# Folding the keys into the query weight in 16 pieces instead of 64, with a new hand-written order of all engines

## The chip, the core and the metric

The kernel runs on one NeuronCore of a Trainium2 chip. The metric is the device time of one execution in microseconds (us). Five engines work side by side: PE (TensorE, matmuls; its weight loads are listed as PEld), DVE (VectorE), ACT (ScalarE), POOL (GpSimd), and SP (SyncE), which here issues every DMA. A matmul reads a stationary operand (the weight) and a moving operand from SBUF and writes PSUM.

## The reference, cut to what matters

S = 2048 tokens of D = 576 features pass through four blocks, A, B, A, B, each with a layer norm in front and a residual sum behind. Both A blocks use the same weights, and so do both B blocks.

```
def A(x):                                   # linear attention, 32 heads of 18
    q, k, v = x @ wqkv
    phi = lambda t: where(t > 0, t + 1, exp(t)) + 1e-6
    kv = phi(k)^T v ;  z = sum over tokens of phi(k)     # per head
    return ((phi(q) kv) / (phi(q) z + 1e-6)) @ wo
def B(x):                                   # 32 heads, 2 x 8 keys of 128, one of 64 experts per head
    q = x @ w_q                             # (tokens, 32, 256)
    s1 = q[..., :128] @ k1.T ; s2 = q[..., 128:] @ k2.T  # 8 scores each
    e = argmax(s1) * 8 + argmax(s2)
    return sum over heads of gelu(x . u[e]) * v[e]
x = x + A(ln(x)); x = x + B(ln(x)); x = x + A(ln(x)); x = x + B(ln(x))
```

The kernel never forms the query of block B. It multiplies w_q by the keys once (the **fold**): 64 blocks of w_q (2 halves of 32 heads, each 128 x 576) times the keys give one 576 x 448 score weight, whose columns are the scores of keys 1 to 7 less that of key 0. Both B blocks use it.

## The kernel before, in words

**Tiles.** The tokens are 16 tiles of 128. For each of the two layers (A and B together, l = 0 and 1) a *front* goes over all tiles: layer norm, transposition (`fT`), and the products with wqkv for k, v and q, each 28 matmuls, because float32 is split into a high and a low part; `st` adds phi(k)^T v of the tile to the state in PSUM. After tile 15 the state is masked (`mk`), summed (`zs`) and multiplied into wo (`M0` to `M4`). Then a *back* goes over all tiles: `num` (POOL and DVE: phi(q) over its denominator), `oT` (transposition), `O` (28 matmuls with the folded wo, residual sum, layer norm), `bT` (transposition), `S` (14 matmuls with the score weight, written into the tile `pps`), `gel` and `sel` (gelu and selection, on ACT, POOL and DVE), `cT` (transposition of the chosen weights, `pc`), and `po` (4 matmuls with v and the residual sum). Most transpositions go through DVE and a round trip to DRAM; a few are on PE. Some q products are left for the back (`q`, or `lq` in layer 1).

**Order.** Nothing is scheduled at run time. A long text is played (`play`, line 719): each word, such as `q0.5` or `F0.12`, names a piece (kind, layer, tile or number), and runs its generator on to its next `yield`; `x2` means two steps. `in_order` (line 136) then ties the instructions of each of PE, ACT, DVE, POOL and SP into the order of the text. So each engine's queue is strictly that order, and a waiting instruction holds back all behind it on its engine.

**The fold.** `wf0.m` (`fold_load`, line 581) issues on SP the load of weight block m (288 KB) into a stage buffer. Stage buffers come in a ring of ten (`RING`, line 110; the tags are shared with tiles of the back), the first 15 uses being the loads of wqkv, so block m waits until block m - 10 has been used. `F0.m` (`fold_mm`, line 585) multiplies one block by the padded keys `kpad`: block m = 16 ch + 4 a + j writes rows 32j to 32j+31 of the PSUM tile `fold_ps` number ch, in two matmuls of 320 and 256 columns. Each is float32 and shows in the trace as two matmul records, so one block is four records. The window of `kpad` shifts with a, so that four a's accumulate into the same rows. `Fo` (ACT) copies a finished chunk ch out, and `FT` transposes and splits it into the score weight `shi`, `slo`; `S` needs all four chunks.

Of the kernel before, what the change touches and what calls it, by code (L numbers as in the profile page):

```python
# [63 lines left out]
def network(ctx, tc, x_in, wqkv, wo, wq_t, k_t, u_t, v2, c_mask, c_mask4, c_ident, c_code, c_code1, c_scale, c_shift, out):  # L64
    nc = tc.nc
# [519 lines left out]
    def fold_mm(l, m):  # L585
        st = fold_st.pop(m)
        ch, i = divmod(m, 16)
        if i == 0:
            fold_ps[ch] = psum(f"fold_ps{ch}")
        p = fold_ps[ch]  # L590
        a, j = divmod(i, 4)
        for c0, c1, at in ((0, 320, 0), (320, D, 512)):
            nc.tensor.matmul(p[32 * j:32 * j + 32, at:at + c1 - c0], kpad[:, ch // 2, 24 - 8 * a:56 - 8 * a],  # L593
                             st[:, c0:c1], start=(a == 0), stop=(a == 3))
# [134 lines left out]
    with in_order(*ALL, ET.SP):  # L729

        play("""
            wu0.2 fi0.0 wk0.0 wu0.14 wk0.1 fi0.0 wk0.3 fi0.0 fl0.0 fl0.1 fi0.0 kl0.0 wk0.4 wf0.0 wk0.0 fl0.2 wk0.2 wk0.0 wk0.1
# [3 lines left out]
            wf0.3 wv0.3 v0.0 k0.1 wf0.4 wq0.3 wf0.5 wf0.6 k0.1 wq0.1x2 ln0.3 v0.1 v0.0 ln0.3 wq0.0 ln0.5 ln0.3 wq0.0 ln0.5 wq0.2
            fl0.7 fT0.3 ln0.5 st0.0 fT0.2 wq0.2 v0.1 q0.0 ln0.4 fT0.3 wf0.7 fT0.5 ln0.4 wf0.8 wf0.9 fl0.10 ln0.4 fT0.5 wf0.10
            fT0.4 fl0.6 F0.2 q0.0 F0.3 st0.1 fT0.4 q0.0 F0.4 q0.1 ln0.7x2 fT0.2 F0.6 F0.1 F0.5 q0.1 wf0.11 fT0.2 k0.2 fT0.3 ln0.7
            q0.1 fT0.7 wf0.12 fl0.14 wf0.13 wf0.14 wf0.15 F0.7 k0.2 fT0.7 F0.9 F0.8 q0.1 v0.2 k0.2 wf0.16 wf0.17 wf0.18 wf0.19
            ln0.10 fT0.5 ln0.10x2 ln0.6 F0.10 q0.0 q0.2 wf0.20 v0.2 fl0.11 fT0.10 ln0.6 fT0.4 ln0.6 fT0.10 fl0.15 fT0.3 st0.2 q0.2  # L740
            fT0.3 F0.12 fT0.6 F0.11 q0.3 wf0.21 ln0.14 wf0.22 fT0.6 q0.2 ln0.14x2 q0.2 fl0.9 F0.14 q0.3 F0.15 wf0.23 F0.13 v0.3
            wf0.24 q0.3 Fo0.0 wf0.25 q0.3 FT0.0 v0.3 F0.16 fT0.14 F0.17 wf0.26 F0.18 FT0.0 k0.3 wf0.27 fT0.7 FT0.0 fT0.5 fT0.14
            wf0.28 fT0.5 F0.19 k0.3 q0.5 wf0.29 k0.3 ln0.11x2 fT0.10 st0.3 ln0.11 F0.20 ln0.15 q0.5 v0.5 wf0.30 fT0.4 fl0.8 q0.5
            fT0.4 k0.4 v0.5 ln0.9x2 F0.21 k0.4 F0.24 wf0.31 F0.22 ln0.9 F0.23 k0.4 wf0.32 k0.5 wf0.33 wf0.34 fl0.13 fT0.9x2
            fT0.11x2 F0.25 k0.5 F0.26 wf0.35 F0.27 v0.4 wf0.36 k0.5 fT0.7 wf0.37 fT0.6 fT0.7 q0.7 v0.4 fT0.10x2 ln0.8 F0.30 q0.7
            F0.28 F0.29 wf0.38 F0.31 q0.7 ln0.8 wf0.39 k0.7 Fo0.1 wf0.40 wf0.41 ln0.8 fT0.8x2 F0.32 F0.34 ln0.13 wf0.42 F0.33
            st0.4 wf0.43 wf0.44 st0.5 q0.7 k0.7x2 q0.4 fl0.12 fT0.9 fT0.11 F0.36 q0.4 F0.35 F0.37 wf0.45 v0.7 ln0.15 ln0.13 ln0.15
            wf0.46 wf0.47 fT0.6x2 ln0.13 F0.39 v0.7 F0.38 F0.40 ld0.1 F0.41 k0.6 wf0.48 wf0.49 fT0.8 F0.42 F0.43 F0.44 q0.4x2 q0.6
            k0.6x2 ln0.12 fT0.9 v0.6 ln0.12 fT0.9 fT0.11 fT0.15 fT0.11 ln0.12 fT0.15 fT0.13 fT0.12 fT0.13 F0.45 v0.6 F0.47 F0.46
            fT0.12 st0.6 Fo0.2 wf0.50 wf0.51 st0.7 wf0.52 q0.6 wf0.53 wf0.54 FT0.2 q0.6 wf0.55 FT0.2 k0.11 fT0.14 FT0.2 q0.6  # L750
            fT0.8x2 k0.8 k0.11x2 fT0.15 fT0.13 v0.8 k0.8x2 fT0.12 q0.8 v0.8 st0.8 v0.11 q0.8x2 fT0.15 q0.8 fT0.15 k0.9 q0.9 k0.9x2
            v0.9 q0.9x3 fT0.12 v0.10 fT0.12 v0.9 q0.12 v0.10 v0.12 q0.12x3 st0.9 v0.11 k0.10x3 k0.12 fT0.13x2 k0.13 k0.12 q0.5
            k0.13 st0.10 k0.12 v0.12 k0.13 v0.13 st0.11 v0.13 st0.12 st0.13 FT0.1x2 k0.15 FT0.1 v0.15 k0.15x2 q0.10 v0.15 fT0.14
            F0.48 q0.10 fT0.14 k0.14 q0.10x2 v0.14 k0.14x2 F0.50 ld0.2 v0.14 F0.54 st0.14 st0.15 mk0.0 zs0.0x2 num0.2x2 F0.49
            F0.53 F0.51 F0.55 wl0.0 F0.52 wl0.0 M0.0 num0.1 q0.15 M0.0x2 num0.2 num0.1 num0.2 num0.1 ld0.0 num0.1 num0.2 M0.3
            q0.15x2 num0.1 wf0.56 M0.1 M0.3 wf0.57 wf0.58 wf0.59 M0.3 M0.1 oT0.1 q0.15 M0.1 oT0.1 num0.0 M0.2 oT0.2 F0.56 M0.2
            M0.4 wf0.60 oT0.1 oT0.2 F0.57 M0.2 oT0.1 wf0.61 M0.4 q0.14 wf0.62 wf0.63 lv0.0 num0.0x3 F0.59 q0.14 F0.60 F0.58 num0.0
            oT0.0 q0.14 O0.1 oT0.2 oT0.0x2 q0.14 oT0.0 F0.61 O0.1 F0.63 F0.62 sv0.0 O0.0 ld0.4 O0.1 Fo0.3 oT0.2 O0.1 oT0.2 FT0.3
            oT0.2 O0.0 O0.1 FT0.3 O0.2 ld0.3 O0.0 num0.4 FT0.3 O0.1 num0.4 O0.0 num0.4x2 bT0.1 S0.1 O0.0 q0.11 bT0.1 O0.2 num0.3
# [130 lines left out]
```

## Time and profile before

| | us |
|---|---|
| median of 3 runs | 770.88 (766.08 to 772.62) |
| the profiled execution: its own time | 769.57 |
| its span, first to last instruction | 767.8 |
| PE busy in the span | 723.3 (94%) |
| DVE / ACT / POOL busy | 492.6 (64%) / 349.0 (45%) / 255.5 (33%) |
| mean granted PE clock | 0.981 |

So 1.8 us of the profiled time lie outside the span. In the views of the profile a line has the start and length in us, the engine, the source line, the operation, its tiles (output <- inputs), the shape and the count, and in brackets the idle time before it and what ended it. Successive matmuls overlap a little, so the time that a stretch of matmuls takes from the queue is the distance from its start to the start of the next stretch; its printed length is a little more.

### The profile page before, as it was taken

The numbers are of one execution on the slowest core, as the hardware profiler recorded it, in microseconds if no ns is written. First come the engines' busy times: TensorE is split into PE (matmuls) and PEld (weight loads), VectorE is DVE, ScalarE is ACT, GpSimd is POOL, SyncE is SP. The second block draws the span as 40 slices with busy tenths as digits, with TensorE's granted clock in tenths as the row PEclk, the third lists the DMA queues.
The fourth block names the chain that finished last, engine by engine and source line by source line (L and its number), as shares of the span: only waits on it lengthen the run. The fifth ranks groups of instructions, "written<-read, shape, count | busy, mean of one in ns | idle before, by whom it ended". The sixth has DMA issues, their size and how long they took to land.

```text
span 767.8 us, 14154 instructions
## 1 busy us (share of the span) xinstructions
PE 723.3 (94%) x4941; PEld 658.8 (86%) x4941; DVE 492.6 (64%) x1041; ACT 349.0 (45%) x709; POOL 255.5 (33%) x586
## 2 busy tenths in 40 slices
...
GB/s 258 302 255 320 133 264 237 211 32 32 1 62 250 141 168 164 205 182 268 227 224 243 201 210 159 199 75 70 161 188 238 217 123 205 124 150 149 180 70 77
DMA packets 112032, 133.92 MB, mean 174 GB/s; under 512 B 12120, under 2 KB 71512, under 8 KB 111960
## 3 DMA queue, kind: packets, MB, share of 16 engines
...
q14 instruction: 33, 0.27, 0.1%
HBM read 82.21 MB, written 50.76 MB: 173 GB/s over the span
## 4 chain that ended last, share of the span: by engine, by line
PE 62%; DVE 14%; POOL 7%; ACT 6%; issue 4%; DMA 4%; SPq 2%; POOLq 0%; ACTq 0%; DVEq 0%
PE ppq L234 13%; PE ppk L234 13%; PE ppv L234 12%; PE pps L474 7%; PE ppo L441 6%; PE fold_ps L593 4%; PE kva L318 3%; SPq L216 2%; PE po L560 1%; POOL o L407 1%; DMA fold<-in_wq_t 1%; DVE m L508 1%; DVE pi L529 1%; ACT junk L169 1%; DVE o L416 1%
## 5 line engine op out<-in xcount | busy, mean ns | idle before, releaser
L407 POOL TENSOR_TENSOR o<-pq,zb 128x576 f32<-128x576 f32 x19 | 27.7, 1459 | 105.5 <-ACT zb L352 96.7
L474 PE MATMUL pps<-shi,thib 128*128 128x512 f32 x160 | 47.0, 427 | 6.7 <-ACT thib L222 3.9
L441 PE MATMUL ppo<-ohi,thio 126*128 126x288 f32 (+1 forms) x320 | 50.4, 299 | 3.0 <-ACT thio L222 2.9
L234 PE MATMUL ppk<-whi,thif 128*128 128x288 f32 x320 | 49.9, 300 | 0.3 <-DVE whi L133 0.2
L234 PE MATMUL ppv<-whi,thif 128*128 128x252 f32 x320 | 48.9, 299 | 0.8 <-ACT thif L198 0.8
L441 PEld LDWEIGHTS ppo<-ohi,thio 126*128 126x128 f32 (+1 forms) x320 | 45.0, 189 | 5.2 <-ACT thio L222 4.0
L234 PE MATMUL ppk<-whi,tlof 128*128 128x288 f32 x320 | 48.6, 296 | 0.1
L234 PE MATMUL ppv<-whi,tlof 128*128 128x252 f32 x320 | 47.9, 295 | 0.0
L234 PEld LDWEIGHTS ppk<-whi,thif 128*128 128x128 f32 x320 | 44.6, 189 | 3.4 <-ACT eq L246 0.8
L234 PEld LDWEIGHTS ppv<-whi,thif 128*128 128x128 f32 x320 | 44.4, 188 | 3.5 <-issue 2.1
L234 PEld LDWEIGHTS ppk<-whi,tlof 128*128 128x128 f32 x320 | 44.6, 188 | 0.3 <-DVE tlof L200 0.3
L234 PEld LDWEIGHTS ppv<-whi,tlof 128*128 128x128 f32 x320 | 44.8, 188 | 0.0
L274 ACT ACTIVATE v<-ppv 128x252 f32<-128x252 f32 x64 | 21.2, 378 | 51.3 <-PE ppv L234 43.8
L474 PE MATMUL pps<-shi,tlob 128*128 128x512 f32 x160 | 43.2, 400 | 0.4 <-DVE tlob L224 0.4
L250 DVE SCALAR_TENSOR_TENSOR ek<-ppk,ek 128x576 f32<-128x576 f32 x32 | 24.2, 756 | 28.6 <-ACT ek L244 26.9
L474 PEld LDWEIGHTS pps<-shi,thib 128*128 128x128 f32 x160 | 30.4, 202 | 13.3 <-ACT thib L222 4.6
L593 PE MATMUL fold_ps<-fold,kpad 128*32 128x320 f32 (+1 forms) x256 | 35.4, 416 | 5.2 <-DMA fold<-in_wq_t 5.2
L441 PE MATMUL ppo<-ohi,tloo 126*128 126x288 f32 x256 | 40.3, 295 | 0.0
L441 PE MATMUL ppo<-olo,thio 126*128 126x288 f32 x256 | 40.2, 295 | 0.0
L234 PE MATMUL ppk<-wlo,thif 128*128 128x288 f32 x256 | 39.8, 295 | 0.0
L234 PE MATMUL ppq<-whi 128*128 128x288 f32 x260 | 39.5, 299 | 0.0
L234 PE MATMUL ppv<-wlo,thif 128*128 128x252 f32 (+1 forms) x256 | 39.3, 295 | 0.0
...
## 6 DMA issues: line engine op xcount, KB each, us to landing
fold<-in_wq_t SPq DMA_DIRECT2D x64, 288.0 KB, 5.1
...
ro<-t_do SPq DMA_DIRECT2D x116, 80.0 KB, 2.2
...
```

Source lines behind the costliest of these rows:

```text
L169: nc.scalar.activation(junk, xt, AF.Square, bias=m[:, 0:1], accum_out=m[:, 1:2])
L216: nc.sync.dma_start(r[32 * a:32 * a + 32].rearrange("r (i e) -> r i e", i=4), t_d[kind, t][:, a * w:(a + 1) * w].rearrange("(i r) e -> r i ...
L234: nc.tensor.matmul(o[:, at:at + c1 - c0], tt[a == "lo"][:, b, :], wb[:, cols + c0:cols + c1], start=(i == 0), stop=(i == len(todo) - 1))
L250: nc.vector.scalar_tensor_tensor(e2, halves(p), 0.0, e2, op0=ALU.max, op1=ALU.add)
L274: nc.scalar.activation(vt[:, c * w:(c + 2) * w].rearrange("p (c e) -> p c e", c=2)[:, :, :HC], x.rearrange("p (c e) -> p c e", c=2), AF.Copy)
L318: nc.tensor.matmul(a[:w, c * HC:(c + 1) * HC], vt[:, c * w:(c + 1) * w], fk[:, c * HC:(c + 1) * HC], start=(t == 0 and c == 0), stop=(t == ...
L407: nc.gpsimd.tensor_tensor(o[:, :D], pq, zb, op=ALU.mult)
L416: nc.vector.tensor_tensor(o[:, :D].rearrange("p (h e) -> p h e", h=H), pq.rearrange("p (h e) -> p h e", h=H), r.unsqueeze(2).to_broadcast( ...
L441: nc.tensor.matmul(p[:, h * 512:h * 512 + HALF], hl[a][:r, b], w[:r, h * HALF:(h + 1) * HALF], start=(i == 0), stop=(i == len(todo) - 1))
L474: nc.tensor.matmul(p[:, :512], hl[a == "lo"][:, b, :], shi[:, b] if w == "hi" else slo[:, blocks(REM)[b][1]], start=(i == 0), stop=(i == l ...
L508: nc.vector.tensor_tensor(m.rearrange("p (e g) -> p e g", e=E), sv, mx.unsqueeze(1).to_broadcast([P, E, NE]), op=ALU.is_ge)
L593: nc.tensor.matmul(p[32 * j:32 * j + 32, at:at + c1 - c0], kpad[:, ch // 2, 24 - 8 * a:56 - 8 * a], st[:, c0:c1], start=(a == 0), stop=(a ...
```

## The change

`fold_mm` takes a number q from 0 to 15 instead of m from 0 to 63, and issues the matmuls of the four blocks 4q to 4q + 3 (j = 0 to 3, one a) one after the other. The number of matmuls, their shapes and operands are the same; nothing else in the functions changes.

```diff
-    def fold_mm(l, m):
-        st = fold_st.pop(m)
-        ch, i = divmod(m, 16)
-        if i == 0:
+    def fold_mm(l, q):
+        ch, a = divmod(q, 4)
+        if a == 0:
             fold_ps[ch] = psum(f"fold_ps{ch}")
         p = fold_ps[ch]
-        a, j = divmod(i, 4)
-        for c0, c1, at in ((0, 320, 0), (320, D, 512)):
-            nc.tensor.matmul(p[32 * j:32 * j + 32, at:at + c1 - c0], kpad[:, ch // 2, 24 - 8 * a:56 - 8 * a],
-                             st[:, c0:c1], start=(a == 0), stop=(a == 3))
+        for j in range(4):
+            st = fold_st.pop(4 * q + j)
+            for c0, c1, at in ((0, 320, 0), (320, D, 512)):
+                nc.tensor.matmul(p[32 * j:32 * j + 32, at:at + c1 - c0], kpad[:, ch // 2, 24 - 8 * a:56 - 8 * a],
+                                 st[:, c0:c1], start=(a == 0), stop=(a == 3))
```

The played text is written anew from the first word to the last. It has the same pieces with the same steps, but for `F0.0` to `F0.63`, which become `F0.0` to `F0.15`. The first words, which hold the first loads:

```diff
-            wu0.2 fi0.0 wk0.0 wu0.14 wk0.1 fi0.0 wk0.3 fi0.0 fl0.0 fl0.1 fi0.0 kl0.0 wk0.4 wf0.0 wk0.0 fl0.2 wk0.2 wk0.0 wk0.1
...
+            wk0.0 kl0.0 wu0.2 fi0.0 wk0.1 wu0.14 fi0.0 wk0.3 fi0.0 fl0.0 fi0.0 fl0.1 wk0.4 wk0.0 fl0.2 kl0.0 wv0.1 wk0.0 wk0.2
...
```

PE's own order from the start to the back of layer 0, read off the old text (layer 0 where no other is written; `F` numbers are blocks):

```
wu wu F0 fT0 fT1 k0 k1 v0 v1 st0 q0 F2 F3 st1 F4 q1 F6 F1 F5 k2 F7 F9 F8 v2 F10 q2 st2 F12 F11 q3 F14 F15 F13 v3
FT0 F16 F17 F18 k3 F19 q5 st3 F20 v5 k4 F21 F24 F22 F23 k5 F25 F26 F27 v4 q7 F30 F28 F29 F31 k7 F32 F34 F33 st4 st5
q4 F36 F35 F37 v7 F39 F38 F40 F41 k6 F42 F43 F44 q6 v6 F45 F47 F46 st6 st7 FT2 k11 k8 v8 q8 st8 v11 k9 q9 v9 v10
q12 v12 st9 k10 k12 k13 st10 v13 st11 st12 st13 FT1 k15 v15 q10 F48 k14 v14 F50 F54 st14 st15 zs F49 F53 F51 F55 F52
M0 q15 M3 M1 oT1 M2 F56 M4 F57 q14 F59 F60 F58 oT0 O1 F61 F63 F62 O0 FT3 O2 bT1 q11 bT0 S1 S0 O4 cT1 O3 cT0 S2 po0 po1
```

and off the new text (`F` numbers are groups of four blocks):

```
wu wu fT0 fT1 k0 k1 v0 v1 st0 st1 q1 q0 k2 F0 F1 v2 q2 v3 F2 F3 k5 q5 k3 FT0 st2 k4 F4 F5 st3 q3 v5 v7 F6 F7 q7 v4
F8 st4 st5 q4 k7 v6 FT1 F9 F10 q6 q9 F11 v9 FT2 k6 v11 st6 st7 q10 v8 k8 v10 st8 k11 k10 k9 q15 st9 st10 st11 k12
v12 q12 st12 v13 v15 k13 k15 st13 k14 v14 F12 st14 st15 F13 zs M0 q8 M3 M1 M4 M2 q14 oT1 F14 oT0 O1 F15 O0 FT3 bT1
q11 S1 bT0 O2 S0 O4 cT1 O3 S2 po1 cT0 po0
```

In layer 0 both texts leave four q products for the back. After the front of layer 1 PE has `zs1 M3 M4 lq3 M2 M1 lq2 M0 lq0 q13 lq1` in the old text, and `lq2 M1 M2 zs1 M4 lq0 M0 lq3 lq1` in the new one, where POOL and DVE begin `num` of layer 1 after `zs1`. The order of the last tiles is nearly the same in both.

More of the change, by code (lines that the diff above doesn't have):

```diff
@@ L736, in network @@
[L736 to L759, printed above, removed]
@@ L816, in network @@
-            q1.15 S1.2 S1.1 sel1.1 gel1.1 bT1.13 gel1.1x3 oT1.6 oT1.4 sel1.1 O1.3 S1.13 S1.2 oT1.6 ldq1.15 sel1.1 oT1.6 bT1.13
-            sel1.1 oT1.4 oT1.14 sel1.1x2 lq1.8 O1.3 num1.15 gel1.2 oT1.4 ldx1.12 O1.3 gel1.2 O1.3 num1.15 oT1.4 rl1.12 oT1.14
-            gel1.2 O1.3 oT1.5 cT1.1 O1.4 O1.3 sel1.2 oT1.5 gel1.2 num1.15 cT1.1 lq1.8 sel1.2 cT1.1 sel1.2 bT1.13 po1.1 bT1.13
-            S1.13 po1.1 sel1.2 po1.1 O1.4 sel1.2x2 bT1.3 S1.3 O1.4 ldx1.14 O1.4 cT1.2 lq1.7 num1.15 bT1.3 S1.13 O1.4 gel1.13
@@ L824, in network @@
-            gel1.3 po1.2 sel1.3 oT1.15 O1.14 num1.9 oT1.8 gel1.3x2 O1.6 S1.4 gel1.3 bT1.14 oT1.7 S1.14 sel1.3 bT1.14 sel1.3 oT1.8
-            lq1.11 sel1.3 oT1.7 sel1.3 bT1.14 sel1.3 gel1.4 O1.6 oT1.7 gel1.4 sel1.4 O1.6 gel1.4 ldx1.5 O1.6 gel1.4 O1.6 cT1.3
-            O1.5 sel1.4 lq1.11 sel1.4 O1.6 lq1.11 bT1.14 sel1.4 cT1.3 bT1.14 S1.14 bT1.6 sel1.4 cT1.3 bT1.6 num1.9 S1.6 sel1.4
-            oT1.8 num1.9 oT1.9 oT1.8 po1.3 S1.14 cT1.4 po1.3 oT1.9 num1.11 gel1.14 O1.7 cT1.4 bT1.6 cT1.4 O1.5 gel1.14 num1.11
@@ L828, in network @@
-            O1.5 gel1.14 ldx1.9 O1.5 gel1.14 po1.3 sel1.14 num1.11 oT1.9 O1.5 po1.4 bT1.6 O1.15 num1.11 O1.5 bT1.6 po1.4 O1.7
-            po1.4 num1.11 sel1.14 ldx1.10 O1.7x2 S1.6 sel1.14 oT1.9 O1.7x2 sel1.14 bT1.5 S1.5 sel1.14x2 bT1.7 bT1.5 cT1.14 lq1.12
-            S1.6 num1.10 bT1.7 cT1.14 gel1.6 sel1.6 num1.10 gel1.6x3 bT1.5 sel1.6 S1.7 O1.8 lq1.12 sel1.6 bT1.7 sel1.6 lq1.12
-            sel1.6x2 bT1.5 num1.10 bT1.5 S1.5 cT1.14 bT1.7 oT1.11 num1.10 oT1.9 num1.12 oT1.10 bT1.7 num1.12 oT1.10 po1.14 S1.5
@@ L844, in network @@
-            cT1.8 po1.8 sel1.9x3 po1.8 sel1.9x2 cT1.9 po1.8 cT1.9x2 po1.9x3
+            wk0.0 kl0.0 wu0.2 fi0.0 wk0.1 wu0.14 fi0.0 wk0.3 fi0.0 fl0.0 fi0.0 fl0.1 wk0.4 wk0.0 fl0.2 kl0.0 wv0.1 wk0.0 wk0.2
+            wk0.1 wv0.3 wv0.4 wk0.1 wk0.3 wv0.0 cd0.0 wk0.3 cd0.0 wv0.2 ln0.0 wq0.0 wq0.3 ln0.1 ln0.0 fi0.0x2 wk0.4 ln0.1 ln0.0
+            fi0.0 fl0.3 fT0.0 ln0.2 ln0.1 fT0.0 fT0.1 fl0.5 wk0.4 ln0.2 wk0.2 fT0.0 wv0.3 wk0.2 k0.0 wq0.1 wq0.4 ln0.2 wv0.3 wq0.2
+            wv0.4 fT0.2 fl0.14 fT0.1 wv0.4 fT0.2 wv0.1 fT0.1 wv0.0 wv0.1 k0.1 wv0.2 wv0.0 k0.0 wq0.0 wv0.2 wq0.3 wq0.0 wq0.3 ln0.3
@@ new lines, in network @@
+            oT0.14 po0.11 k1.7 fT1.9x2 fT1.10 S0.12 oT0.14 fT1.10 gel0.12 po0.11 sel0.12 gel0.12 bT0.15 oT0.14 gel0.12 fT1.8
+            gel0.12 fT1.11 S0.15 fT1.11 sel0.12 O0.14 k1.7 fT1.9 sel0.12 fT1.10 bT0.15 sel0.12 k1.7 sel0.12x2 bT0.15 cT0.12 fT1.11
+            st1.6 cT0.12 fT1.9 O0.14 st1.7 cT0.12 O0.14 fT1.8 O0.14 keep1.8 po0.12 O0.14 po0.12 O0.14 bT0.14 po0.12x3 bT0.14
+            po0.12 ldx1.2 po0.12 fT1.12x2 bT0.14 fT1.12 S0.13 k1.8 S0.13 gel0.13 fT1.10 sel0.13 gel0.13x2 v1.8 gel0.13 k1.8
@@ new lines, in network @@
+            O1.13 oT1.14 S1.1 O1.13 num1.4 ldx1.5 oT1.3 O1.13 oT1.6 bT1.1 num1.4 O1.13 num1.4 bT1.2 oT1.14 cT1.0 bT1.2 O1.13 po1.0
+            oT1.5 S1.1 q1.15 num1.4 bT1.13 oT1.5 oT1.6 oT1.4 bT1.13 q1.15 S1.2 S1.1 oT1.6 q1.15 gel1.1x2 sel1.1 oT1.6 gel1.1
+            bT1.13 oT1.14 gel1.1 sel1.1 O1.3 S1.2 S1.13 sel1.1 oT1.14 bT1.13 sel1.1 oT1.14 sel1.1 lq1.8 ldq1.15 oT1.4 num1.15
+            po1.0 O1.3 po1.0 oT1.4 bT1.13 num1.15 sel1.2 num1.15 rl1.12 sel1.1 O1.3 gel1.2 cT1.1 lq1.8 S1.13 gel1.2 sel1.2 ldx1.4
@@ new lines, in network @@
+            sel1.2 O1.3 sel1.2 oT1.4 O1.3 lq1.7 lq1.8 gel1.2 O1.3 gel1.2 num1.15 num1.8 cT1.1x2 sel1.2 S1.13 bT1.3 rl1.11 oT1.4
+            S1.3 num1.15 po1.1 lq1.7 num1.8 oT1.4 O1.4 bT1.3 sel1.2 po1.1 num1.8 sel1.13 po1.1 gel1.13x2 sel1.13 cT1.2 lq1.9 bT1.3
+            O1.4 lq1.7 O1.4x2 sel1.13 ldx1.6 O1.4 sel1.13 O1.4 oT1.15 lq1.10 bT1.3 bT1.4 oT1.15 num1.7 sel1.13 lq1.9 num1.8 bT1.4
+            bT1.3 num1.7 gel1.13 lq1.9 cT1.2 oT1.15 O1.14 lq1.10 num1.7 cT1.2 gel1.13 num1.7 S1.4 num1.8 bT1.4 num1.7 oT1.8
@@ new lines, in network @@
+            sel1.13 lq1.10 num1.9 oT1.8 oT1.15 oT1.7 cT1.13 po1.2 cT1.13 S1.3 num1.9 num1.10 oT1.7 cT1.13 oT1.15 num1.9 oT1.8
+            po1.2 bT1.4 oT1.15 O1.14 po1.13 S1.3 bT1.4 oT1.7 O1.6 po1.13 gel1.3 sel1.3 O1.14x2 po1.2 ldx1.10 O1.14 oT1.8 sel1.3
+            S1.4 po1.13 gel1.3 O1.14 sel1.3 gel1.3x2 sel1.3 bT1.14 sel1.3x2 oT1.7 O1.6 bT1.14 lq1.11 S1.14 S1.4 oT1.7 O1.6 ldx1.9
+            gel1.4 sel1.4 oT1.7 O1.6x2 bT1.14 sel1.4 cT1.3 O1.6 oT1.8 O1.5 num1.9 oT1.8 cT1.3 lq1.11 bT1.6 num1.9 cT1.3 bT1.6
@@ new lines, in network @@
+            sel1.4 bT1.14 po1.3 gel1.4x2 bT1.14 S1.14 lq1.11 sel1.4 gel1.4 bT1.6 oT1.9 sel1.4 S1.6 sel1.4 po1.3 num1.11 O1.5 oT1.9
+            cT1.4 O1.7 cT1.4 po1.3 S1.14 cT1.4 O1.5 ldx1.7 num1.11 O1.5 sel1.14 num1.11 bT1.6 O1.5 gel1.14 oT1.9 num1.11 gel1.14
+            O1.5 po1.4 bT1.6 S1.6 gel1.14 bT1.5 po1.4 bT1.5 gel1.14 sel1.14 num1.11 S1.5 oT1.11 S1.6 O1.7 sel1.6 O1.7 ldx1.12
+            O1.7x2 sel1.14 O1.7 sel1.14 num1.10 sel1.14x2 gel1.6 sel1.6x2 O1.8 oT1.11 lq1.12 bT1.5 po1.4 oT1.11 num1.10 gel1.6
```

162 lines of the change are left out of this document (87 added, 75 removed).

## Prediction

> **What bounds the kernel now.** I read the page's busy times first, then its chain, then the costliest groups.
>
> ```profile
> PE 723.3 (94%) x4941; PEld 658.8 (86%) x4941; DVE 492.6 (64%) x1041; ACT 349.0 (45%) x709; POOL 255.5 (33%) x586
> ...
> PE 62%; DVE 14%; POOL 7%; ACT 6%; issue 4%; DMA 4%; SPq 2%; POOLq 0%; ACTq 0%; DVEq 0%
> ...
> L593 PE MATMUL fold_ps<-fold,kpad 128*32 128x320 f32 (+1 forms) x256 | 35.4, 416 | 5.2 <-DMA fold<-in_wq_t 5.2
> ```
>
> PE is busy for 94% of the span and holds 62% of the chain; the fold is 35.4 us of that. Whether PE time removed comes off the end depends on the stage, so next the busy time by stage (stretch, its length, then busy us of each engine, clock, DMA share, GB/s):
>
> ```profile
> 0.00:20.00 20.00, 13.41 (x56) 7.80 (x57) 10.11 (x21) 10.20 (x14) 6.78 (x22) 0.91 0.86 263
> 20.00:220.00 200.00, 200.00 (x1535) 183.51 (x1534) 76.80 (x145) 59.98 (x131) 15.75 (x39) 1.00 0.54 173
> 220.00:260.00 40.00, 39.10 (x263) 30.55 (x262) 20.48 (x39) 12.35 (x25) 8.02 (x16) 1.00 0.58 172
> 260.00:300.00 40.00, 31.86 (x191) 28.47 (x190) 33.54 (x70) 16.30 (x36) 19.64 (x45) 0.91 0.51 151
> 300.00:540.00 240.00, 235.88 (x1653) 224.85 (x1652) 170.18 (x370) 137.50 (x286) 92.34 (x227) 1.00 0.60 190
> 540.00:660.00 120.00, 115.98 (x791) 110.21 (x790) 92.81 (x183) 66.29 (x116) 57.44 (x117) 1.00 0.62 185
> 660.00:767.80 107.80, 87.09 (x466) 73.42 (x464) 88.73 (x217) 46.35 (x104) 55.57 (x121) 0.91 0.40 123
> ```
>
> From 20 to 220 PE never rests: each us taken from its queue there is a us off the end of layer 0's front, if its inputs still come in time. All fold work lies before 257. Behind it PE idles 8.1 us between 260 and 300, and 20.7 us after 660; in between it is nearly full.
>
> **The fold's real price.** A stretch costs the distance from its start to the next one's. From three stretches of PE's timeline:
>
> ```profile
> 36.38 1.17 PE L593 MATMUL fold_ps<-fold,kpad 128*32 128x320 f32 x8
> 37.48 1.15 PE L318 MATMUL kva<-ek,v 128*127 128x126 f32 x8
> ...
> 43.70 2.14 PE L593 MATMUL fold_ps<-fold,kpad 128*32 128x320 f32 x12
> 45.77 1.60 PE L234 MATMUL ppk<-whi,thif 128*128 128x288 f32 x10
> ```
>
> ```profile
> 76.41 1.16 PE L593 MATMUL fold_ps<-fold,kpad 128*32 128x320 f32 x4
> 77.50 1.60 PE L234 MATMUL ppq<-whi,thif 128*128 128x288 f32 x10
> ...
> 91.18 1.20 PE L593 MATMUL fold_ps<-fold,kpad 128*32 128x320 f32 x16
> 92.31 1.60 PE L234 MATMUL ppk<-whi,thif 128*128 128x288 f32 x10
> ...
> 96.24 1.18 PE L593 MATMUL fold_ps<-fold,kpad 128*32 128x320 f32 x12
> 97.35 1.59 PE L234 MATMUL ppv<-whi,thif 128*128 128x252 f32 x10
> ```
>
> ```profile
> 227.59 1.16 PE L349 MATMUL z<-kvb,pick 127*128 127x126 f32 x8 [0.38 <-DVE kvb L340]
> ...
> 228.85 3.16 PE L593 MATMUL fold_ps<-fold,kpad 128*32 128x320 f32 x20
> 231.94 1.24 PE L367 MATMUL m<-wob,kvb 126*126 126x288 f32 x4
> ```
>
> One block (x4) takes 1.09 us, two (x8) 1.10, three (x12) 1.11, four (x16) 1.13. Blocks of different j, which write different rows of `fold_ps`, cost hardly more than one. Where two of one stretch share a j they do not: blocks 6, 1 and 5 (x12 at 43.70) have j = 2, 1, 1 and take 2.07; 49, 53, 51, 55, 52 (x20) have j = 1, 1, 3, 3, 0 and take 3.09, three passes of 1.03. So the unit of cost is the pass over the array, not the block.
>
> The timeline has 26 stretches in all: seven of one block at 1.09 (7.6), two of two at 1.10 (2.2), ten of three at 1.11 (11.1), three of four at 1.13 (3.4), two of two passes (2.07 + 2.06), the one of 3.09, and the first (2.02, below): 33.6 us. The group's 35.4 is the same sum with some 0.07 of overlap at each end. What follows a stretch is also slower:
>
> ```profile
> 82.51 1.09 PE fold_ps L593 x4
> 83.60 3.92 PE ppv L234 x28
> 87.52 3.73 PE ppk L234 x28
> ```
>
> In the chain, the product right behind a fold takes 3.92 and the next 3.73: 0.2 per stretch for the change of form, 26 x 0.2 = 5.2. The fold before: **38.8 us of PE's queue**.
>
> **After.** Sixteen groups, j = 0 to 3 each, so 16 passes. In the new order ten of them stand as five pairs with nothing between (F0 F1, F2 F3, F4 F5, F6 F7, F9 F10) and six alone: 11 stretches. A pair has two passes; 2.07 at 43.70, with 0.03 for fuller passes: 2.1. So 5 x 2.1 + 6 x 1.13 + 11 x 0.2 = 10.5 + 6.8 + 2.2 = **19.5 us**. Removed: 19.3.
>
> Two deductions at the start:
>
> ```profile
> 11.54 2.09 PE L593 MATMUL fold_ps<-fold,kpad 128*32 128x320 f32 x4 [4.98 <-DMA fold<-in_wq_t]
> 13.56 1.98 PE L194 MATMUL ptf<-ident,yf 128*128 128x128 f32 x10
> ```
>
> ```profile
> 10.50 1.93 ACT L182 ACTIVATE yf<-xf,rsf 128x640 f32<-128x640 f32 x2
> ```
>
> ```profile
> 2.59 0.91 SPq L634 DMA_DIRECT2D xf<-in_x  x2
> 3.54 0.43 SPq L645 DMA_DIRECT2D kraw<-in_k_t  x1
> ```
>
> Block 0 is gone from ahead of the transpositions, but the 4.98 us wait before it is not won: the first yf ends about 11.5 (half of the two from 10.50), so they could hardly start sooner. The 2.02 was at the slow clock of the first slice (0.91 on average; the same x4 is 1.09 later); that slowness now falls on the first product, so I count 1.1, not 2.0. And `kl0` now issues the key load ahead of the first tiles' loads: one place on SP, 3.54 - 3.06 (half of the 0.91 pair) = 0.5. Together 1.4: **17.9 us left**.
>
> Where it falls: up to the last `st` of the front 21 stretches (26.1 + 4.2) become eight (13.9 + 1.6): 14.8, less the 1.4, so 13.4. The rest falls between z and O0.1, which was 22.5 us (227.59 to 250.09):
>
> ```profile
> 250.09 1.58 PE L441 MATMUL ppo<-ohi,thio 126*128 126x288 f32 x10
> ```
>
> There 3.09 and three single stretches (7.2 with the changes of form) become one of 1.3, while F13 stands before z: 5.9 us sooner after z, 17.9 in all. PE holds 15 us of other work (M, two q products) to cover `num`, whose transposition came 11.5 us after z:
>
> ```profile
> 239.11 0.74 PE L194 MATMUL pto<-ident,o 128*128 128x128 f32 x5 [0.25 <-DVE eq L250]
> ```
>
> so O0.1 should not wait. Everything else is the same work; for the new order beyond the fold I take 0, with bounds of 8 us gained (the idle of 260 to 300) and 6 us lost (below). No wait is added in the code, but a group now needs four loads; SP issues them and holds the transposition transfers behind a load that waits for its buffer:
>
> ```profile
> fold<-in_wq_t SPq DMA_DIRECT2D x64, 288.0 KB, 5.1
> ```
>
> ```profile
> SPq L583 <- PE fold_ps L593: 29.7, 9, 8.0
> ```
>
> Before, SP waited 29.7 us for folds to free buffers (nine times, 8.0 at most), and yet PE lost only 5.2 to fold loads (the group's row), nearly all of it the first wait. A pair frees eight of ten buffers at once; the shortest PE work from such a release to the next need is F0 F1 to F2 (v2 q2 v3: 11.2 us) and F9 F10 to F11 (q6 q9: 7.5, plus a pass), against 5.1 us of landing and 0.43 per issue (the key load's row). Eight loads (2.3 MB) at the 320 GB/s that a busy slice moved need 7.2:
>
> ```profile
> 60.00:80.00 20.00, 20.00 (x152) 16.64 (x151) 8.89 (x21) 5.95 (x16) 1.24 (x5) 1.00 0.98 320
> ```
>
> Tight but inside; I take 0, bounds 0 and 41 (eight waits of 5.1).
>
> Sum: 769.57 - 17.9 = 751.7 against the profiled time, which lies 1.3 below the median; **753** against the median.
>
> **Rivals.**
> *The ramp gives part of it back* (759). Between 260 and 300 DVE is the fullest engine (33.54 of 40) and PE waits:
>
> ```profile
> 290.80 0.47 PE L456 MATMUL pc<-ident,cg 128*128 128x128 f32 x1 [6.26 <-POOL cg L541]
> ```
>
> If selection paces that ramp from zs on, the 5.9 us won between zs and O0.1 turn into a longer wait there: 753 + 6. Against it: the new order puts S2 and po1 ahead of that transposition, and before 260 DVE was half idle (20.48 of 40), so an earlier O feeds it earlier. Chance 0.18.
>
> *The late order loses* (759, with the ramp 765). In layer 1, zs now stands behind one q product and M1, M2, where it came at once:
>
> ```profile
> 538.81 1.16 PE z L349 x8
> ...
> 540.14 1.99 PE m L367 x8
> ```
>
> That is 3.7 + 2.0 us later, and `num` with it; from 660 on DVE and PE are equally full (88.73 and 87.09 of 107.8), so late DVE work can show at the end. For it: PE's 20.7 idle there; against: from 540 to 660 PE has 116.0 of 120, so the q products left for then cover a late `num`. Chance 0.12.
>
> *The loads gate PE* (slower). With both pairs and the ring, each of the eight stretches up to F12 waits for a fourth load: at 5.1 each 41 us, 753 + 41 = 794. It decides from 26 us on, when five of the eight waits are whole. For it: DMA 0.98 busy at 60 to 80; against: by v7 the new order has asked for 24 blocks where the old had done 38. Whole 0.05; in part, 763 to 778, 0.11.
>
> *Four abreast cost more than the three x16 stretches say.* If a group took a third of the way from the one-pass row (1.13) to the two-pass row (2.07), 1.44, then 16 x 0.31 = 5.0 us would be lost: 758. Against it, the row itself: 4 x 1.09 / 1.13 is 3.9 times the rate of one block. Chance 0.03.
> The Trainium skill has such a figure: "TensorE: Matmul & The Clock Gate", section Part 3: Packing small matmuls, gives a measured gain of 3.07 for four row tiles and 2.38 for three column tiles; at 3.07 a group would take 4 / 3.07 x 1.09 = 1.42 and the sum would come to 757.6. The trace, with 3.9 on column tiles, does not agree, and I follow the trace.
>
> *The change does more*: the new order also closes the 8.1 us of idle in the ramp, 745. Chance 0.05.
>
> **How the numbers follow.** Forecast (748 to 757) 0.46, ramp 0.18, late order 0.12, loads in part 0.11, loads whole 0.05, packing 0.03, more 0.05. The range, 745 to 766, takes in all but the loads whole, most of the loads in part and a little at the low end: 0.17 out. One per cent is 7.7 us, about what a measurement of this kernel can tell from no change, so faster means under 763.2: forecast, more, packing, ramp, and the late order without its worst 0.02, together 0.82. Same: loads in part and that 0.02, 0.13. Slower: 0.05.
>
> **What would show it.** The fold group still x256, but in 11 stretches of about 1.13 or 2.1 start to start, and some 18 us in the group instead of 35.4. PE full from about 18 us to the end of the front, which comes some 13 us earlier; O0.1 and the end some 18 earlier. Wrong if PE's fold groups wait for `fold` loads by more than 3 us in sum, if the idle after 260 grows by more than 5 us over 8.1 + 4.1 + 4.0 + 20.7, or if groups take 1.4.

## The result, and the profile after

| | before | after |
|---|---|---|
| median, runs side by side | 768.48 us (761.85 to 772.62, 4 runs) | 738.72 us (737.36 to 739.41, 4 runs) |
| the profiled execution / its span | 769.57 / 767.8 | 737.36 / 735.5 |
| PE busy / PE idle in the span | 723.3 / 44.5 | 704.8 / 30.7 |

The ratio is 0.9618, 95% interval 0.9542 to 0.9694. The change is faster, by 32 us in the profiled executions, where 18 were forecast; 738.7 lies below the range of 745 to 766.

The page of the changed kernel, busy times; two groups of PE, the fold and the transposition `pc` (busy us, mean ns | idle before, and what ended it); the busy time by stage, in the stretches shown before:

```profile
PE 704.8 (96%) x4941; PEld 654.4 (89%) x4941; DVE 493.0 (67%) x1041; ACT 350.1 (48%) x709; POOL 253.7 (34%) x586
```

```profile
L593 PE MATMUL fold_ps<-fold,kpad 128*32 128x256 f32 (+1 forms) x256 | 20.4, 411 | 0.4 <-DMA fold<-in_wq_t 0.3
...
L456 PE MATMUL pc<-ident,cg 128*128 128x128 f32 x32 | 9.5, 300 | 6.4 <-POOL cg L541 4.0 <-DVE x L430 1.6 <-ACT g L491 0.8
```

```profile
0.00:20.00 20.00, 14.66 (x62) 10.24 (x63) 11.83 (x24) 12.01 (x17) 7.21 (x22) 0.83 0.91 251
20.00:220.00 200.00, 200.00 (x1634) 190.63 (x1633) 78.52 (x152) 60.52 (x134) 17.41 (x42) 1.00 0.57 181
220.00:260.00 40.00, 38.55 (x251) 32.24 (x250) 30.69 (x60) 18.76 (x37) 12.92 (x35) 1.00 0.63 194
260.00:300.00 40.00, 35.73 (x230) 33.10 (x228) 37.85 (x82) 23.28 (x49) 24.09 (x57) 0.96 0.64 204
300.00:540.00 240.00, 239.34 (x1691) 229.87 (x1690) 165.54 (x349) 136.78 (x277) 83.55 (x205) 1.00 0.59 187
540.00:660.00 120.00, 119.42 (x799) 112.78 (x798) 109.42 (x231) 69.39 (x131) 73.24 (x148) 1.00 0.65 195
660.00:735.50 75.50, 57.09 (x288) 45.58 (x286) 59.17 (x149) 29.35 (x67) 35.25 (x80) 0.90 0.35 112
```

The fold's group has shrunk from 35.4 to 20.4 us. PE is full from 20 to 220 as before, and between 300 and 660 it now idles 1.2 us where it idled 8.1. The group's row gives 0.3 us of PE idle for late loads, but that is not all that they cost: see the last group below.

The fold and the two marks of the forecast, z and O0.1, on PE's timeline after:

```profile
13.79 0.84 PE L234 MATMUL ppk<-whi,thif 128*128 128x288 f32 x2
...
43.60 2.19 PE L593 MATMUL fold_ps<-fold,kpad 128*32 128x320 f32 x32
45.77 1.60 PE L234 MATMUL ppv<-whi,thif 128*128 128x252 f32 x10
...
213.69 1.20 PE L593 MATMUL fold_ps<-fold,kpad 128*32 128x320 f32 x16
214.81 1.16 PE L349 MATMUL z<-kvb,pick 127*128 127x126 f32 x8
...
231.12 1.57 PE L441 MATMUL ppo<-ohi,thio 126*128 126x288 f32 x10
...
235.03 2.40 PE L593 MATMUL fold_ps<-fold,kpad 128*32 128x320 f32 x12
237.77 1.16 PE L593 MATMUL fold_ps<-fold,kpad 128*32 128x320 f32 x4 [0.34 <-DMA fold<-in_wq_t]
```

The last group takes 3.8 us from start to start (235.03 to 238.85), where every other single group takes 1.12 or 1.13. PE's weight loads of its third and fourth block waited for `fold`:

```profile
236.27 0.14 PEld L593 LDWEIGHTS fold_ps<-fold,kpad 128*32 128x32 f32 x2 [0.55 <-DMA fold<-in_wq_t]
...
237.77 0.14 PEld L593 LDWEIGHTS fold_ps<-fold,kpad 128*32 128x32 f32 x2 [0.82 <-DMA fold<-in_wq_t]
```

So it ran as three passes in place of one, and late loads cost PE 2.7 us there, most of which the profile counts as busy.

z comes 12.8 us earlier (227.59 to 214.81), O0.1 19.0 earlier (250.09 to 231.12), the end of the span 32.3 earlier. So 13.3 us are won behind O0.1, where the forecast had put nothing.

To find them I cut each span at its own events, and took PE's idle time of each piece (its length less PE's busy time in the busy-by-stage view cut there): start to first product, front to z, z to O0.1, the *ramp* (50 us behind O0.1), the *middle* (on to the z of layer 1), the *late* part (120 us behind that), and the tail.

| PE idle, us | start | front | z to O0.1 | ramp | middle | late | tail | sum |
|---|---|---|---|---|---|---|---|---|
| before | 6.3 | 0.6 | 0.5 | 8.1 | 4.1 | 4.0 | 20.7 | 44.5 |
| after | 5.3 | 0 | 0 | 5.2 | 1.2 | 0.2 | 18.8 | 30.7 |

Behind O0.1 the idle time fell from 37.0 to 25.4: 11.6 of the 13.3. It is spread over all four pieces. The other 1.7 is busy time. One place where busy time went is the ramp, on PE's timeline before:

```profile
290.92 2.48 PE L474 MATMUL pps<-shi,thib 128*128 128x512 f32 x5
293.20 1.85 PE L474 MATMUL pps<-slo,thib 128*128 128x512 f32 x4
294.90 1.32 PE L474 MATMUL pps<-shi,tlob 128*128 128x512 f32 x5
```

and after:

```profile
266.15 2.77 PE L441 MATMUL ppo<-ohi,thio 126*128 126x288 f32 x10 [2.26 <-ACT thio L222]
...
271.48 1.33 PE L474 MATMUL pps<-shi,thib 128*128 128x512 f32 x5
272.65 1.09 PE L474 MATMUL pps<-slo,thib 128*128 128x512 f32 x4
...
276.38 0.33 PE L456 MATMUL pc<-ident,cg 128*128 128x128 f32 x1 [0.94 <-POOL cg L541]
```

Before, the scores of tile 2 stood behind the transposition that waited 6.26 us for POOL's `cg`, and then ran at half the clock (2.48 for what takes 1.33; the granted clock is 0.50 from 290.8 to 294). After, they run ahead of it, and the wait is 0.94; a wait of 2.26 stands earlier, and the products behind it start at half the clock (2.77 for ten).

### The profile page after: what moved, and what is told of

Same layout as the page of the kernel before. It is cut to its first block, busy times and chain, and to the rows that moved or that the text cites. A ratio compares the mean times of both kernels' runs of the same rounds, so it can differ in the third digit from the quotient of the medians.

```text
span 735.5 us, 14140 instructions
## 1 busy us (share of the span) xinstructions
PE 704.8 (96%) x4941; PEld 654.4 (89%) x4941; DVE 493.0 (67%) x1041; ACT 350.1 (48%) x709; POOL 253.7 (34%) x586
## 5 line engine op out<-in xcount | busy, mean ns | idle before, releaser
L474 PE MATMUL pps<-shi,thib 128*128 128x512 f32 x160 | 43.7, 403 | 2.0 <-ACT thib L222 1.3
L182 ACT ACTIVATE yb<-x,rsb 128x640 f32<-128x640 f32 x32 | 29.5, 921 | 20.5 <-POOL rsb L174 20.5
L474 PEld LDWEIGHTS pps<-shi,tlob 128*128 128x128 f32 x160 | 30.3, 191 | 9.2 <-DVE tlob L200 1.5
```

What stands on the lines that cost most here:

```text
L182: nc.scalar.activation(y, x2, AF.Identity, scale=rs[:, 0:1], bias=rs[:, 1:2])
L474: nc.tensor.matmul(p[:, :512], hl[a == "lo"][:, b, :], shi[:, b] if w == "hi" else slo[:, blocks(REM)[b][1]], start=(i == 0), stop=(i == l ...
```

## The experiments

"Old" and "new" are the two texts. A mixed order runs one text up to a named step, and then the steps of the other that are still to be done, in that one's order. Medians of the kernel before beside these runs were 766.74 (the first four), 767.01 (the next four) and 765.23 (the last four), so that across them ratios are the better measure; each has its interval.

### The groups in the old order

```diff
-F0.1 ... F0.63      (each block at its own place)
+F0.0 ... F0.15      (each group where the old text has its last block; groups 12 to 14 at another of theirs)
 (some block loads later, where a buffer comes free; all else is the old text)
```

> The old order of all engines, with the fold in 16 groups of four blocks side by side; a group stands where the last of its four blocks stood (groups 12 to 14 a little earlier), loads and back tiles that would have no free buffer a little later. Theory A (the forecast's sum was right for the fold, and the new order gave the rest): the fold takes 16 x (1.13 + 0.2) = 21.3 us of PE in place of 38.8, so about 17 us off the old kernel's 768.5, 752 +- 4, and PE idle outside the fold stays near 40 us. Theory B (the whole gain is the fold's, and the order is neutral): about 740, PE idle near 31.

754.12 us (750.30 to 754.99), ratio 0.9837 (0.9793 to 0.9881). A. PE's timeline:

```profile
39.92 1.20 PE L593 MATMUL fold_ps<-fold,kpad 128*32 128x320 f32 x16
41.05 1.20 PE L234 MATMUL ppk<-whi,thif 128*128 128x288 f32 x7
...
240.04 1.20 PE L593 MATMUL fold_ps<-fold,kpad 128*32 128x320 f32 x16 [1.36 <-DMA fold<-in_wq_t]
...
276.55 0.48 PE L456 MATMUL pc<-ident,cg 128*128 128x128 f32 x1 [5.98 <-POOL cg L541]
```

Sixteen stretches at 1.13, O0.1 15.4 us earlier (234.7) and the end 14.6 (span 753.2): what the fold gives goes through to the end but for 0.8. The ramp's wait is there as before, at 5.98, and the ramp's idle time is 9.2 us where it was 8.1. So the groups alone are 12.6 us of the 30 by medians (14.6 by spans, where about 17 were expected), and the order is the rest: 15.4 us by medians (754.12 to 738.72), 17.0 against the changed kernel's second median below.

### The new order up to the first state, and up to the second

```diff
 new text up to mk0.0 (the state of layer 0), old text behind
 (q0.8 and q0.15, ld0.0 and ld0.2 trade places; a load of the last group waits for its buffer)
```

> The new order up to the mask of layer 0's state, the old order behind it, with groups in both (q0.8 and q0.15, ld0.0 and ld0.2 trade places in the first part so that what is left over fits). Theory A: the front ends as in the new kernel (z near 214 us), but the ramp, the middle, layer 1's late part and the tail take the old idle back: 8.1 + 4.1 + 4.0 + 20.7 = 36.9 of PE idle behind z against 25.4 in the new kernel, so 738.7 + 11 = 750. Theory B: 740.

749.24 us (749.02 to 750.46), ratio 0.9786 (0.9750 to 0.9823). A. The ramp on PE:

```profile
275.09 0.47 PE L456 MATMUL pc<-ident,cg 128*128 128x128 f32 x1 [6.38 <-POOL cg L541]
275.22 2.48 PE L474 MATMUL pps<-shi,thib 128*128 128x512 f32 x5
```

```diff
 new text up to mk1.0 (the state of layer 1), old text behind
 (ldx1.3 and ldx1.4 trade places)
```

> The new order up to the mask of layer 1's state, the old order behind it (ldx1.3 and ldx1.4 trade places in the first part). Theory A: only the late part and the tail take their old idle back, 24.7 us in place of 19.0: 738.7 + 5.7 = 744.5. Theory B: 739. If late parts depend on what they find and not on their own order, also 739.

742.73 us (741.65 to 742.79), ratio 0.9694 (0.9651 to 0.9737). A, at its low side. So by medians the order is worth 4.9 us in the front (1.8 of it the five stretches that become pairs, by the prediction's prices), 6.5 in ramp and middle, and about 4 behind the second state; by ratios 3.9, 7.1 and 5.7. PE's idle in the ramp and middle falls from 9.5 + 4.2 to 5.0 + 1.8, which is 7.0. The late part, 120 us from 20 us behind z; first with the old late order, then the changed kernel's row as shown above for 540 to 660:

```profile
534.00:654.00 120.00, 116.80 (x788) 110.22 (x787) 100.76 (x213) 66.92 (x123) 67.56 (x140) 1.00 0.61 186
```

DVE does 100.8 us of work there, with the new late order 109.4, and PE 116.8 against 119.4: less is left for the tail.

### Five passes for one

```diff
-        for j in range(4):
-            st = fold_st.pop(4 * q + j)
+        for again in range(5 if a == 0 else 1):
+            for j in range(4):
+                st = fold_st[4 * q + j]
...
```

The first group of each chunk is multiplied five times. Each time starts the sum anew (`start` is set where a is 0), so the score weight stays what it was.

> The new kernel, in which the first group of each chunk (F0, F4, F8, F12) is multiplied five times in place of once, each time from the start: sixteen more passes over the array, all in layer 0's front, nothing else changed. Both theories, if PE time in the front comes off the end one to one: 16 x 1.03 = 16.5 us, 755. If later waits absorb a part (or a later front makes later waits longer): less (or more) by that part. Per pass it also gives the price of a pass: by the trace of before 1.03 us, 66 ns by four blocks each hardly dearer than one.

751.38 us (750.33 to 752.98), ratio 0.9813 (0.9775 to 0.9851); span 751.2, which is 15.7 more than the changed kernel's.

```profile
43.49 6.10 PE L594 MATMUL fold_ps<-fold,kpad 128*32 128x320 f32 x96
49.52 1.60 PE L234 MATMUL ppv<-whi,thif 128*128 128x252 f32 x10
```

Six passes take 6.03 us from start to start, about 1 each, as the prediction had it, and z of layer 0 comes 15.5 later (214.8 to 230.3). Sixteen more cost 12.7 by medians (14.2 against the changed kernel's second median, below) and 15.7 by the spans. So most of the 15.5, by the spans all of it, shows at the end.

### The changed kernel again, and the late order on the old middle

> The changed kernel once more, unedited, so that the runs beside it are compared with it on one chip. Every theory says 738.7, within 2; its distance to the unchanged kernel 28 to 30 us.

737.14 us (734.96 to 739.11, 6 runs), ratio 0.9620 (0.9588 to 0.9652): 29.9 us under the kernel before beside it.

```diff
 old text, with groups, up to mk1.0, new text behind
 (ldx1.3 and ldx1.4 trade places)
```

> The old order of steps, with the sixteen groups, up to the state of layer 1, and the new order behind it. Theory A: the gains of the stretches of the order add up, and the late order is worth 4.0 us (742.7 - 738.7) whatever stands ahead of it: 754.1 - 4.0 = 750, PE's idle of the 120 us behind the second z under 1 us (2.79 with the old late order). Theory B: the late order only keeps what the new middle hands it (data ready earlier), and behind the old middle it is worth nothing: 754, that idle still 2 to 4 us.

752.82 us (748.81 to 755.79), ratio 0.9823 (0.9787 to 0.9859): between the two, and not to be told from the groups alone. The late part does as A says (PE idle 0.4). But at the cut a wait is added:

```profile
529.08 2.74 PE L234 MATMUL ppq<-whi 128*128 128x288 f32 x10 [4.23 <-DMA whi<-hl_d]
531.62 2.12 PE L234 MATMUL ppq<-wlo,whi 128*128 128x288 f32 x8
```

The new late order begins with the query product of tile 2, whose operand is reloaded into the columns of wv, so not before the last v product. The new middle puts four tiles of state between that product and this one, the old middle only two. The products behind the wait are slow too (2.74 for ten; the granted clock is 0.50 from 529 to 532). So this run can't say what the late order is worth by itself; it shows that behind the old middle it pays for a wait that the new middle covers.

### The ramp's wait, mended in the old order

```diff
-... S0.4 sel0.0 ... sel0.0x2 cT0.0 bT0.2 num0.5 S0.2 cT0.0 ...
+... S0.4 bT0.2 sel0.0 ... sel0.0x2 S0.2 cT0.0 num0.5 cT0.0 ...     (the kernel with the new front)
```

> The kernel with the new order only up to the state of layer 0 (749.2; old order behind it), in which three steps are moved: the scores of tile 2 on PE go ahead of the transposition of tile 0's weights, which waited 6.38 us there for POOL's cg, and the last DVE step of tile 2's turning goes ahead of the last of tile 0's selection. Nothing else. Theory A: the loss at that place is its order on PE: 4.88 us of scores (2.28 + 1.41 + 1.16 start to start, the first at a slow clock) now run inside the wait, selection is 0.9 us later for the DVE step, so 4 us come off: 745, the wait for cg under 3 us, and the scores at 3.5 us instead of 4.9. Theory B: selection paces the ramp, and what PE does ahead of it comes back as another wait behind it: 749, with the same idle of PE in the 50 us behind O0.1 (9.5).

750.16 us (745.28 to 751.15), ratio 0.9779 (0.9740 to 0.9817), against 0.9786 without it: nothing, B. PE in the ramp:

```profile
270.90 1.43 PE L474 MATMUL pps<-shi,thib 128*128 128x512 f32 x5 [2.25 <-ACT thib L222]
...
275.79 0.33 PE L456 MATMUL pc<-ident,cg 128*128 128x128 f32 x1 [1.36 <-POOL cg L541]
277.47 0.53 PE L560 MATMUL po<-vmix,chi 128*128 128x288 f32 x2 [1.35 <-DVE clo L461]
...
279.42 0.82 PE L560 MATMUL po<-vmix,clo 128*128 128x288 f32 x2 [0.89 <-DVE clo L461]
280.04 2.60 PE L441 MATMUL ppo<-ohi,thio 126*128 126x288 f32 x10
```

The wait of 6.38 has become four, 5.85 together, and the half clock has moved to the next product. PE's idle in the 50 us behind O0.1 did fall, from 9.5 to 8.0, but none of it shows at the end.

```diff
+ cT0.1 (its clo on DVE) and po0.1 (PE and DVE) also ahead of cT0.0; fT1.1 ahead of the scores of tile 4
```

> The kernel of the moved scores (750.2, where moving the scores ahead of the wait for cg gave nothing) with one tile more carried through: tile 1's clo on DVE, which the old order put 14 us behind its chi, its output on PE (po) and the sum behind it go ahead of the wait too, and the transposition that begins layer 1 for it comes ahead of the scores of tile 4, as in the new order. Theory A: the ramp loses because tile 1, which opens layer 1 and with it a large store of PE work, is held behind tile 0: layer 1's first product, at 290.1 there, comes at about 286, PE's idle of the 50 us behind O0.1 falls from 8.0 towards the 5.2 of the new order, 746 to 747. Theory B: nothing short of the whole order helps: 750.

750.95 us (748.50 to 751.86), ratio 0.9799 (0.9767 to 0.9831): B again. My guess that tile 1 held up layer 1 fell; layer 1's first product starts at 291.8, not at 286:

```profile
285.50 0.77 PE L194 MATMUL ptf<-ident,yf 128*128 128x128 f32 x5 [3.36 <-ACT yf L182]
286.02 2.13 PE L474 MATMUL pps<-shi,thib 128*128 128x512 f32 x5
```

The waits for cg and clo are gone, that of 2.25 stays, and one of 3.36 for the layer norm of tile 1 has come in their place.

### The same place, undone in the new order

```diff
-... S0.2 num0.5 ... po0.1 sel0.0 S0.2 ... sel0.0 sel0.2 num0.5 gel0.2 cT0.0x2 ...
+... num0.5 ... sel0.0 cT0.0 S0.2 po0.1 S0.2 sel0.2 num0.5 gel0.2 cT0.0 ...      (the changed kernel)
```

> The changed kernel with one place of the ramp put back as the old order has it: on PE the transposition of tile 0's weights, which waits for cg, goes ahead of the scores of tile 2 and of tile 1's output (and what hangs on these behind it). Theory A: PE then waits some 4 to 5 us more at that place (cg comes at about 276, PE arrives at 271.5), and tile 1 is late for layer 1: 737.5 + 4 to 5 = 742. Theory B, from the run in which moving the scores gave nothing: the wait moves and the end does not, 738.

743.23 us (741.96 to 744.78), ratio 0.9702 (0.9671 to 0.9733), against 0.9620: about 6 us lost, A. PE's timeline, and its busy time and clock (the third number from the end of a row) around the place:

```profile
277.09 0.48 PE L456 MATMUL pc<-ident,cg 128*128 128x128 f32 x1 [3.15 <-POOL cg L541]
277.22 2.48 PE L474 MATMUL pps<-shi,thib 128*128 128x512 f32 x5
```

```profile
266.00:270.00 4.00, 2.75 (x11) 2.75 (x12) 3.90 (x11) 2.34 (x4) 2.60 (x7) 0.56 0.77 225
270.00:274.00 4.00, 3.94 (x19) 3.70 (x17) 3.93 (x7) 0.92 (x1) 1.85 (x4) 0.59 0.50 183
274.00:277.00 3.00, 0.00 (x0) 0.00 (x0) 2.66 (x6) 0.26 (x1) 1.24 (x3) 0.95 0.70 174
277.00:280.00 3.00, 2.91 (x8) 2.33 (x9) 0.00 (x0) 0.00 (x0) 0.21 (x2) 0.50 0.12 28
```

The first two rows lie ahead of the moved step, behind a wait of 2.30 for `thio`. The changed kernel has that wait too (2.26), and then this clock:

```profile
266.00:270.00 4.00, 3.85 (x17) 3.85 (x18) 3.90 (x9) 2.63 (x5) 2.29 (x6) 0.57 0.62 182
```

From 270 on its clock is 1.00 again. So the first 26 products behind that wait take 6.3 us here and 5.1 there, and some 1 us of what this profile lost is not the step's. The step's own part is the wait of 3.15, where it was 0.94, and the half clock behind it.

Taken out of the order in which it pays, the step costs; put into the other order, it gives nothing.

### The new ramp alone

```diff
 new text up to keep1.1 (the transposition of layer 1's first tile, about 282 us), old text behind
```

> The new order up to the end of the ramp (until the first tile of layer 1 is transposed, about 282 us), the old order behind it. In the kernel with the new front alone the ramp idled 9.53 us of PE and the middle 4.23; with the new order up to the second state 4.99 and 1.76 and 6.5 us less in the end. Theory A: ramp and middle are worth what PE's idle in each says: here the ramp falls to 5.0 and the middle stays at 4.2, 749.2 - 4.5 = 744.7. Theory B: the middle's idle hangs on what the ramp hands it, and both fall: 742.7. Theory C: what the ramp saves comes back in the middle (selection paces both): 749.

747.88 us (745.45 to 749.21), ratio 0.9757 (0.9721 to 0.9792): 2.2 us better than the new front alone by the ratios (1.4 by medians), between C and A and nearer C. PE's idle in the ramp did fall, from 9.5 to 5.7, but the middle's rose from 4.2 to 5.5. What PE waited for between 282 and 520 (us in total, times, longest):

```profile
PE po L560 <- DVE clo L461: 1.7, 2, 1.1
PE pc L456 <- POOL cg L541: 1.5, 4, 0.6
PE po L560 <- ACT chi L459: 0.9, 1, 0.9
```

These are small waits for the chosen weights of single tiles. With the old ramp ahead of the same middle they are 1.0, 0.9 and 0.3; in the changed kernel the second of them is 0.6 and the others do not show.

### The late part

```diff
 the changed kernel, with zs1.0 directly behind mk1.0, ahead of lq1.2, M1.1 and M1.2
```

> The changed kernel with one thing put back as it was before: in layer 1 the sum of the state (z) stands ahead of the query product of tile 2 and of M1 and M2, its copy zb behind that product's start. My rival of the prediction (the late order loses, because z and with it num come 5.7 us later): 738.7 - 5.7 = 733, or half of it, 736, where the tail hides a part. Theory now: the first num waits for its own query product, which z now delays by 1.3 us and by what z waits for the masked state: 738.7 to 740, and the first POOL product of layer 1 no earlier than 7.9 us behind the end of the state's products.

738.07 us (736.72 to 740.79), ratio 0.9635 (0.9604 to 0.9667): no change. PE's z, here and then in the changed kernel:

```profile
514.50 1.16 PE L349 MATMUL z<-kvb,pick 127*128 127x126 f32 x8 [0.38 <-DVE kvb L340]
```

```profile
520.13 1.05 PE L349 MATMUL z<-kvb,pick 127*128 127x126 f32 x8
```

POOL's first product of layer 1, here and then in the changed kernel:

```profile
522.69 1.43 POOL L407 TENSOR_TENSOR o<-eq,zb 128x576 f32<-128x576 f32 x1 [37.17 <-DVE eq L250]
```

```profile
522.26 1.42 POOL L407 TENSOR_TENSOR o<-eq,zb 128x576 f32<-128x576 f32 x1 [36.27 <-ACT zb L352]
```

With z 5.6 us earlier, `num` starts no earlier (522.69 and 522.26): it then waits for the query product of its own tile, `eq`.

```diff
 new text up to lq1.11 (about 620 us), old text behind
```

> The new order up to the query product of tile 11 in layer 1 (about 620 us), the old order behind it. The late order was worth 4.0 us. Theory A: it earns this by keeping DVE at work (37 to 38 of 40 us between 560 and 640, against 34 to 35 with the old late order) and PE without idle there: 738 to 739 here, whatever the last 110 us do. Theory B: it is the order of the last tiles in the tail: 741 to 742.

739.81 us (738.08 to 743.11), ratio 0.9659 (0.9625 to 0.9693). It lies half way between the changed kernel (0.9620) and the one with the old late order (0.9694): neither theory is whole, and the late order's gain is split about evenly between the two halves, as far as these intervals tell.

## Why the prediction was right and wrong

**The fold: right.** The 17.9 us for the fold came out as 19.0 at O0.1. Single groups take 1.12 to 1.13 and pairs 2.11 to 2.17 from start to start; only the last group was split by late loads (3.8 us, behind O0.1), for which the busy time is 20.4 and not "some 18". Of the 1.1 us more, half came at the start. The first product begins 1.9 earlier (15.68 to 13.79) but runs its first matmuls at a slow clock, as the prediction had it (0.51 from 14 to 17), so that the first v product is 1.3 earlier (24.03 to 22.74); the fold's first stretch, the change of form and the deduction of 1.4 left 0.8. The rest was not traced; PE idled 0.6 us in the front and 0.5 between z and O0.1 before, and not at all after. That this time comes off the end was the reading of the full stretch of 20 to 220, and the groups alone (14.6 at the end for 15.4 at O0.1) and the added passes bear it out.

**"For the new order beyond the fold I take 0, with bounds of 8 gained and 6 lost": the term that failed.** It was 13.3 in the profiled executions. The run with the groups alone agrees: it leaves 15.4 to 17.0 us by medians for the order, of which 1.8 are the pairs that the fold's sum had already counted. Two things were wrong in the term. The upper bound took the idle time of one window, 260 to 300, while the idle time behind O0.1 was 37.0 us (8.1, 4.1, 4.0, 20.7; the prediction lists these numbers, but only as a test that they should not grow). An order that is new from the first word to the last can work on all of it. And the most likely value, 0, had no row behind it, though the trace of before had one that spoke against it:

```profile
PE pc L456 <- POOL cg L541: 13.4, 8, 6.3
```

PE's waits for `cg` alone were 13.4 us, eight of them, and the order sets where such a wait stands; after, they are 4.0. The bound should have been the idle time that the order can reach, and the value somewhere inside it. How much of it a written order would recover I could not work out from the trace of before; even with both texts at hand, single places mended in the old order gained nothing (the next point).

**"The ramp gives part of it back": wrong**, and the argument against it, that S2 and po1 stand ahead of the transposition, was too simple. In the old order of steps the ramp did give back about 1 us (its idle time went from 8.1 to 9.2 with the groups alone), not 6. The place matters in the new order (undoing it costs about 6), but mending it in the old one moved the wait into four others. The ramp's data come through a chain of POOL, ACT and DVE steps for several tiles at once. The new order has moved many of them together, and which of the moves pay is not shown; DVE does 37.9 of 40 us from 260 to 300 where it did 33.5.

**"The late order loses": wrong in its premise.** It had `num` wait for z. z was the last to come only because it had been put behind; with z back in front nothing changes. The late order gains 4 to 6 (medians and ratios), with DVE kept busier.

**The loads: nearly right at 0; four abreast: right.** The groups of the front lost next to nothing, but the last one lost 2.7 us to its loads, against a bound of 41 and a sign of being wrong at 3. The prediction looked for the shortest PE work between a release of buffers and the next need, and left out the one from F14 to F15: SP issues these loads at 230.60, right behind F14, and PE comes to F15 at 235.03, 4.4 us later, against 5.1 of landing. In the old order of steps the last group waited 1.36. Whether the 2.7 us reach the end is not shown. The 1.13 of three rows held for all single groups whose loads were there, and pairs take two such passes.

**"The change does more", 0.05, 745:** the right direction with a wrong size, for it too counted only the ramp.

**What stays open.** Front, ramp and middle, and late part are told apart, but not additive: the new ramp without its middle brings 2.2 us, with it some 7; the late order on the old middle adds a wait. Which steps of the middle depend on the new ramp was not taken apart further.

## What to carry to other kernels

When a change rewrites the order of an in-order queue, price it apart from the work it removes: its upper bound is about all the idle time of the bottleneck engine behind the first moved step, with what a slow clock behind its waits costs, not that of the window that looks worst. A long wait at one place does not mean that the place is the loss: move what waits and see whether the idle time goes or only splits up. And a block that is multiplied by few columns is cheapest beside others that write other rows of the same tile: four cost what one does (1.13 us against 1.09 here).

## What the chip showed

A PE wait of only 2.3 us can be followed by several us at half the clock. In the changed kernel, behind the wait of 2.26, the granted clock is 0.57 over four us, and ten matmuls take 2.77 instead of 1.58. In the run with the place undone it is 0.56 and 0.59 over the 8 us around and behind the wait of 2.30, and 0.50 over three us behind the wait of 3.15. It need not be so: in the run with the scores moved ahead, a wait of 2.25 is followed by four us at the full clock (1.00; the scores' first five matmuls take 1.43), and half the clock comes only after three more waits of 0.9 to 1.4. So a wait in the ramp can cost one to three us beyond its own length, and orders that differ in few waits can differ in busy time. What decides whether the clock is halved is not worked out here. The Trainium skill, "TensorE: Matmul & The Clock Gate", Part 1: The HAM clock gate, gives about 3.4 us of idle time until the clock is halved; here 2.26 us were enough (2.6 with the one transposition ahead of them), so the trace agrees with the halving and not with the length.
